# One layer's last two Strassen products, taken as a two-level unit

## The chip, the core and the metric

The kernel runs on one core of a Trainium2 chip. A core has a matmul engine (TensorE, `PE` in the profile, with its weight loads as `PEld`), a vector engine (VectorE, `DVE`), an activation engine (ScalarE, `ACT`), GpSimd (`POOL`) and a sync engine (`SP`), which in this kernel issues nearly all DMAs. Each engine runs its own instructions in order, and semaphores tie the engines together. The metric is the time of one launch in microseconds (us), as the median of several runs; a profiled execution gives the trace.

## The reference

Linear attention, then a block that mixes with Fourier transforms and a feed-forward layer, all in float32 (8 sequences of 576 tokens, 512 wide):

```python
def _attn_ref(q, k, v):                       # 8 heads of 64
    q_s = softmax(q, axis=-1); k_s = softmax(k, axis=2)
    kv = np.einsum('bhsd,bhse->bhde', k_s, v)
    return np.einsum('bhsd,bhde->bhse', q_s, kv)

def _moe_ref(x, w_ch1, w_ch2):                # w_ch1 512 x 2048, w_ch2 2048 x 512
    mixed = np.real(np.fft.fft(np.fft.fft(x, axis=1), axis=2))
    u = x + mixed
    un = (u - mean(u)) / np.sqrt(var(u) + 1e-06)
    return u + np.maximum(un @ w_ch1, 0.0) @ w_ch2
```

## The kernel before

The tokens are worked through in nine groups of 512, called orders. Order 0 multiplies plainly. From order 1 on the two layers of the feed-forward part are multiplied by Strassen's scheme in Winograd's form: seven products of half-size blocks take the place of eight, and sums of blocks are made before (the left and the right sides) and after. The products are numbered as in `A_AT` and `B_AT`, which say which of the seven left and right blocks each takes, and run in the order `ORDER = (1, 6, 5, 7, 2, 4, 3)`. While order 1 runs through its layers, TensorE also does the attention and the Fourier mixing of later sequences, and the other engines norm the tokens of the group that follows (`norm`: statistics L1335 and L1336, scales L1354 and L1357, normed tokens L1373, transposes on VectorE L1396, their pieces laid out by ScalarE and GpSimd L1404, and the right sides L1410, L1414, L1419).

Order 1's second layer is `down`. Its left side is the hidden layer: 512 tokens by 2048, seven blocks (slots) of 256 tokens by 1024 in the tile `big`. Each product is 16 matmuls of 128x128 by 128x256 (L2055; two records each in the trace), into one of three PSUM banks: 1 and 2 into `ba`, 6, 7 and 4 into `bb`, 5 and 3 into `bc`. `strassen` reads the banks: after product 1 ScalarE copies `ba` to `s1` (L1529); after 6 and 7 VectorE makes `u2` and `u3` from `bb` and `s1` (L1528); after 7, 2, 4 and 3 it adds a bank into a quarter of the tokens' tile x (L2070). GpSimd adds `s1`, `u2` and `u3` into x as well (L2065). So product 2 ends with the x add from `ba`, product 4 with that from `bb`, product 3 with that from `bc`.

The right side is seven combinations of the layer's weights, each a chunk of 1 MB loaded from DRAM (`w2s`) into a ring of four buffers in `big` (L490). `used(n)` frees chunk n and issues the load of chunk n + 4. Behind order 1's seven chunks in this ring come the first-layer chunks of order 2 (`w1s`, 896 KB each).

Orders 2 and later use a second level of Strassen in this layer (`deep_down`): products are taken in pairs, a unit, and each product is seven sub-products of 4 matmuls of 128x128 by 128x128 (L1938). The second combinations of the weights that this needs are made once, during order 1: for each product m but 1, `deepen` takes m's chunk, makes four sums (weights 4 and 1 on VectorE, 5 and 6 on GpSimd, L1818) into a spare place, and stores seven blocks to DRAM (`w2d`, 256 KB each, L1824): the three raw ones at once, the four sums six steps later. The spare place is in turn the gap behind the hidden layer (`gap`) and the slot of the product that has just been done.

The order of the work is a list. Every step is recorded with a time in a unit of its own (one product of this layer is 8 units), the list is sorted by these times, and each engine gets its instructions in that order; so a step written earlier comes earlier on its engine's queue, whatever it then waits for. In the layer, `deepen` starts at 8 for product 6, 12 for 5, 24 for 7, 28 for 2, 40 for 4 and 44 for 3. The products fill units 0 to 56, and order 2 starts at 56 (`UP`). The stores of x follow the x adds (`store`).

Of the kernel before, what the change touches and what calls it, by code (L numbers as in the profile page):

```python
# [52 lines left out]
HD = D // 2  # L53
# [26 lines left out]
ORDER = (1, 6, 5, 7, 2, 4, 3)  # L80
# [4 lines left out]
UP, TWICE = NP * len(ORDER), 8 + 6 * len(ORDER)  # L85
# [39 lines left out]
def at(t, script):  # L125
    return [(t + dt, step) for dt, step in script]
# [17 lines left out]
class _Block:  # L144
# [1365 lines left out]
            second.append(steps)  # L1510
        return first, second

    def strassen(self, product, step, out, early=lambda *a: []):

        nc, V = self.nc, self.nc.vector
        box = {}

        def bank(n):  # L1520
            box[n] = self.ps.tile([P, 2, HD], F32, tag=n, name=n)

        def temp(n):
# [4 lines left out]
        plus = lambda t: V.tensor_tensor(out=temp(t), in0=box["bb"][:], in1=box["s1"][:], op=ALU.add)  # L1528
# [508 lines left out]
    def down(self, g, order):  # L2037
        if order > 1:
            return self.deep_down(g, order)
        nc, V = self.nc, self.nc.vector  # L2040
        h = [self.hpairs(p) for p in range(NP)]
        steps, t = [], 4 * 2
        for k, m in enumerate(ORDER):
            if m != 1:
                spare = [self.hblock(A_AT[ORDER[k - 1]], a, b) for a in range(2) for b in range(2)]
                n = self.base[order] + NP + k
                steps += at(t * k - 4 * (k % 2 == 0), self.deepen(m, n, spare if k % 2 else [self.gap(i) for i in range(4)]))

        def product(m, bank, first):
            n = self.base[order] + NP + ORDER.index(m)  # L2050

            def run(i, q):
                w = self.stream[n]
                for p in range(4 * q, 4 * q + 4):
                    nc.tensor.matmul(bank()[:, i, :], lhsT=h[p][:, A_AT[m], i * P:(i + 1) * P], rhs=w[:, p, :],  # L2055
                                     start=first and i == 0 and p == 0, stop=p == NP - 1,
                                     skip_group_check=True)
                if (i, q) == (1, 1):
                    self.used(n)
            return [lambda i=i, q=q: run(i, q) for i in range(2) for q in range(2)]  # L2060

        def early(i, j, t):
            u, d = i - 1 if (i, j) != (1, 2) else 0, j - 1
            x = lambda: self.xs[g, u][:, :, d * HD:(d + 1) * HD]
            return [(0, lambda: nc.gpsimd.tensor_tensor(out=x(), in0=x(), in1=t()[:], op=ALU.add))]  # L2065

        def out(u, d, store):
            def run(bank, t):
                x = lambda: self.xs[g, u][:, :, d * HD:(d + 1) * HD]
                steps = [(0, lambda: V.tensor_tensor(out=x(), in0=bank()[:], in1=x(), op=ALU.add))]  # L2070
                for c in range(2 * store):
                    steps += at(15 + c, self.store(g, c, u, lambda c=c: self.xpart(g, c, u)))
                return steps
# [55 lines left out]
def kernel(ctx: ExitStack, tc: tile.TileContext, q, kT, v, w1, w2, ft,  # L2129
# [3 lines left out]
    ups = lambda order: 3 * UNIT + 2 * len(SHORT) * (NP // 2) if order in WIDE else UP  # L2133
# [61 lines left out]
    first, second, both = 46.9, 56, 77  # L2195
    steps = blk.opening(fetch, converted)
# [3 lines left out]
    t = first + second  # L2200
    for i, some in enumerate(down):
        steps += at(t + 1.2 * i, some)
# [93 lines left out]
```

## Time and profile before

| | before |
|---|---|
| median of 3 runs | 1002.66 us (1002.32 to 1003.45) |
| the profiled execution | 1004.02 us, its span 1002.1 us |
| TensorE busy | 990.0 us, 99% of the span |
| VectorE / ScalarE / GpSimd busy | 746.5 / 500.1 / 506.0 us |
| order 1's second layer on TensorE | from 229.75 us to 283.93 us |
| DMA | 240.32 MB, mean 240 GB/s |

A row of a timeline has the start in us from the start of the span, the length in us, the engine, the line, the operation, what is written from what, shapes, how many instructions of the same kind follow each other, and in brackets how long the engine stood idle before and what ended it. A row of several spans from the first's start to the last's end. Rows of windows give, for a stretch, the busy time and the number of instructions of PE, PEld, DVE, ACT and POOL, then the granted clock, the DMA share and GB/s. A row of waits has the total, how often, and the longest. `SPq` is the queue that issues DMAs.

### The profile page before, as it was taken

The numbers are of one execution on the slowest core, as the hardware profiler recorded it, in microseconds if no ns is written. First come the engines' busy times: TensorE is split into PE (matmuls) and PEld (weight loads), VectorE is DVE, ScalarE is ACT, GpSimd is POOL, SyncE is SP. The second block draws the span as 40 slices with busy tenths as digits, with TensorE's granted clock in tenths as the row PEclk, the third lists the DMA queues.
The fourth block names the chain that finished last, engine by engine and source line by source line (L and its number), as shares of the span: only waits on it lengthen the run. The fifth ranks groups of instructions, "written<-read, shape, count | busy, mean of one in ns | idle before, by whom it ended". The sixth has DMA issues, their size and how long they took to land.

```text
span 1002.1 us, 20374 instructions
## 1 busy us (share of the span) xinstructions
PE 990.0 (99%) x7754; PEld 856.9 (86%) x7754; DVE 746.5 (74%) x1402; ACT 500.1 (50%) x1290; POOL 506.0 (50%) x498
## 2 busy tenths in 40 slices
PE   8999999999999999999999999999999999999998
PEld 6845464888888899889988998899888999999997
DVE  6898899666765887678756886678657866895793
ACT  5585643872468228842775267724782243251310
POOL 4263420357535637664656556564647398352610
PEclk9999999999999999999999999999999999999999
DMA  9987499687989666975769577947656874677473
GB/s 301 261 282 245 161 253 339 199 245 224 332 295 270 225 233 224 253 256 202 265 196 241 210 263 246 260 175 260 231 174 230 311 251 153 251 268 246 151 268 140
DMA packets 128040, 240.32 MB, mean 240 GB/s; under 512 B 24312, under 2 KB 92152, under 8 KB 117448
## 3 DMA queue, kind: packets, MB, share of 16 engines
q1 hardware_dynamic: 127576, 238.51, 73.0%
q8 instruction: 61, 1.00, 0.4%
q14 instruction: 35, 0.29, 0.1%
q10 hardware_dynamic: 288, 0.26, 0.1%
q0 software_dynamic: 80, 0.26, 0.1%
HBM read 203.87 MB, written 39.06 MB: 242 GB/s over the span
## 4 chain that ended last, share of the span: by engine, by line
PE 87%; DVE 7%; DMA 2%; ACT 2%; issue 1%; SPq 0%; POOL 0%; DVEq 0%; POOLq 0%
PE bb L1560 12%; PE bb L1938 10%; PE ba L1560 8%; PE bc L1560 8%; PE ba L1938 7%; PE bc L1938 7%; PE bb L1888 4%; PE bc L1493 2%; PE bb L2055 2%; PE two L854 2%; PE one L769 2%; PE two L1221 1%; PE two L1278 1%; PE ba L1493 1%; PE ba L1716 1%; PE bc L2055 1%
## 5 line engine op out<-in xcount | busy, mean ns | idle before, releaser
L1560 PE MATMUL bb<-unT,big 128*128 128x256 f32 x576 | 137.8, 381 | 0.0
L1560 PEld LDWEIGHTS bb<-unT,big 128*128 128x128 f32 x576 | 108.4, 190 | 15.6 <-DVE u L1528 0.5
L831 ACT ACTIVATE qT<-q 32x128 f32<-32x128 f32 x384 | 117.9, 307 | 5.9 <-DVE q L821 0.7
L1938 PE MATMUL bb<-big 128*128 128x128 f32 x832 | 101.8, 276 | 0.2 <-DVE u L1945 0.2
L1938 PEld LDWEIGHTS bb<-big 128*128 128x128 f32 x832 | 97.1, 192 | 1.0 <-DVE u L1945 1.0
L1560 PE MATMUL ba<-unT,big 128*128 128x256 f32 x384 | 93.7, 383 | 0.7 <-DMA big<-w1s 0.7
L1560 PE MATMUL bc<-unT,big 128*128 128x256 f32 x384 | 91.2, 380 | 0.1
L1868 POOL TENSOR_TENSOR x<-x,big 128x512 f32<-128x512 f32 x45 | 60.7, 1362 | 45.9 <-DVE big L1945 19.7
L1572 ACT ACTIVATE big<-big 128x512 f32<-128x512 f32 x72 | 44.7, 628 | 78.2 <-DVE big L1571 71.6
L1560 PEld LDWEIGHTS bc<-unT,big 128*128 128x128 f32 x384 | 72.5, 190 | 10.4 <-DVE big L1571 0.5
L1528 DVE TENSOR_TENSOR u<-bb,s 128x512 f32<-128x512 f32 x50 | 34.2, 683 | 63.3 <-PE bb L1560 46.3
L1560 PEld LDWEIGHTS ba<-unT,big 128*128 128x128 f32 x384 | 71.3, 190 | 11.4 <-DMA big<-w1s 0.8
L1938 PE MATMUL ba<-big 128*128 128x128 f32 x648 | 80.1, 276 | 0.0
L1864 DVE TENSOR_TENSOR big<-big 128x512 f32<-128x512 f32 x95 | 78.1, 847 | 0.0
L1938 PEld LDWEIGHTS ba<-big 128*128 128x128 f32 x648 | 75.9, 192 | 0.8
L818 POOL TENSOR_TENSOR q<-q,qm 128x512 f32<-128x512 f32 x24 | 25.8, 1074 | 90.6 <-DVE qm L813 56.9
L1404 POOL COPY unT<-unT 32x256 f32<-32x256 f32 x98 | 43.5, 444 | 46.6 <-DVE unT L1396 42.3
L1404 ACT COPY unT<-unT 32x256 f32<-32x256 f32 x126 | 50.7, 402 | 29.8 <-DVE unT L1396 28.0
L415 POOL TENSOR_TENSOR big<-big 128x512 f32<-128x512 f32 x24 | 30.5, 1270 | 66.6 <-ACT big L1572 66.6
L1938 PE MATMUL bc<-big 128*128 128x128 f32 x400 | 48.9, 275 | 0.0
L1888 PE MATMUL bb<-big 128*128 128x256 f32 x208 | 47.7, 379 | 0.0
L1938 PEld LDWEIGHTS bc<-big 128*128 128x128 f32 x400 | 46.8, 192 | 0.0
(457 smaller groups left out, 2252.4 us busy)
## 6 DMA issues: line engine op xcount, KB each, us to landing
big<-w2d SPq DMA_DIRECT2D x68, 1024.0 KB
big<-w1s SPq DMA_DIRECT2D x64, 896.0 KB
big<-w2s SPq DMA_DIRECT2D x14, 1024.0 KB
big<-in_w_dram SPq DMA_DIRECT2D x21, 512.0 KB
w2d<-big SPq DMA_DIRECT2D x42, 256.0 KB
kb<-in_kT_dram SPq DMA_DIRECT2D x28, 320.0 KB
q<-in_q_dram SPq DMA_DIRECT2D x28, 256.0 KB
vt<-in_v_dram SPq DMA_DIRECT2D x84, 80.0 KB
```

Source lines behind the costliest of these rows:

```text
L415: e1.tensor_tensor(out=to(4), in0=at(2), in1=at(3), op=ALU.add)
L831: nc.scalar.activation(to[t, i * Q:i * Q + Q], one, ACT.Exp)
L1404: copy(to, of)
L1493: nc.tensor.matmul(po[:], lhsT=h[:, f, i * P:(i + 1) * P], rhs=self.w2sb[:, f, :], start=(f == 0), stop=(f == NF - 1))
L1528: plus = lambda t: V.tensor_tensor(out=temp(t), in0=box["bb"][:], in1=box["s1"][:], op=ALU.add)
L1560: nc.tensor.matmul(bank()[:, i, :], lhsT=w[:, WA_AT[m], k * P:(k + 1) * P], rhs=self.unT[g][:, B_AT[m], k, :], start=first and i == 0 and ...
L1572: (0.8, lambda: nc.scalar.activation(hp(i), hp(i), ACT.Relu))]
L1864: (engine or e).tensor_tensor(out=to(o), in0=to(x), in1=to(y), op=op)
L1868: E.tensor_tensor(out=x, in0=x, in1=tile(m), op=ALU.add)
L1888: nc.tensor.matmul(box[name][:, i, :], lhsT=h[p][:, A_AT[m], i * P:(i + 1) * P], rhs=self.stream[n][:, p, :], start=p == 0 and (m != 1 or ...
L1938: nc.tensor.matmul(box[place(unit, n)][:, i, :], lhsT=own(m)(A_AT[n])[:, f, :], rhs=w[:, r // 2, r % 2 * P:r % 2 * P + P], start=first and ...
L2055: nc.tensor.matmul(bank()[:, i, :], lhsT=h[p][:, A_AT[m], i * P:(i + 1) * P], rhs=w[:, p, :], start=first and i == 0 and p == 0, stop=p == ...
```

## The change

Products 4 and 3 of order 1's second layer are taken together as one two-level unit, `last_pair`, of the kind that later orders have: 7 sub-products by 2 by 4 matmuls of 128x128 by 128x128. Its right side is what `deepen` has made for products 4 and 3, still in its spare place, and the raw blocks of the chunks; its left side gets four sums for each of the two products, written into slots 0 and 5 (`dead`). Sub-products 1 and 2 go into `bb`, 6, 7 and 4 into `ba`, 5 and 3 into `bc`. The results are written over the hidden layer's slots 3 and 6, and GpSimd adds them into x (`into`).

The weights' sums of `deepen` start at 8 (product 6), 12 (5), 18 (7), 25 (4), 28 (2) and 33 (3), with other spare places. The x adds from `bb` and `bc` that ended products 4 and 3 come right after product 7, without those products. Chunks 4 and 3 are freed at the end of the unit. Order 2 starts two units earlier, and the stores of x have times of their own. On VectorE the sums 4, 4, 5, 5 of the left side stand before the x add from `ba`.

```diff
-    def strassen(self, product, step, out, early=lambda *a: []):
+    def strassen(self, product, step, out, early=lambda *a: [], order=ORDER):
...
-        for m in ORDER:
+        if 4 not in order:
+            ends[7] += at(0.1, out[2, 1](get("bb"), None) + out[1, 2](get("bc"), None))
+        for m in order:
...
-        steps, t = [], 4 * 2
+        steps, t, spare = [], 4 * 2, {}
         for k, m in enumerate(ORDER):
             if m != 1:
-                spare = [self.hblock(A_AT[ORDER[k - 1]], a, b) for a in range(2) for b in range(2)]
-                n = self.base[order] + NP + k
-                steps += at(t * k - 4 * (k % 2 == 0), self.deepen(m, n, spare if k % 2 else [self.gap(i) for i in range(4)]))
+                dead, start = {6: (1, 8), 5: (0, 12), 7: (6, 18), 4: (5, 25), 2: (0, 28), 3: (7, 33)}[m]
+                spare[m] = [self.hblock(A_AT[dead], a, b) if dead else self.gap(2 * a + b) for a in range(2) for b in range(2)]
+                steps += at(start, self.deepen(m, self.base[order] + NP + k, spare[m]))
...
-        return steps + self.strassen(product, 2, {(1, 1): out(0, 0, False), (2, 1): out(1, 0, True),
-                                                  (2, 2): out(1, 1, False), (1, 2): out(0, 1, True)}, early)
+        for c in range(4):
+            steps += at((62.5 if c < 2 else 70.5) + c % 2, self.store(g, c % 2, c < 2, lambda c=c: self.xpart(g, c % 2, c < 2)))
+        return steps + at(t * 5, self.last_pair(g, order, spare)) + self.strassen(
+            product, 2, {(1, 1): out(0, 0), (2, 1): out(1, 0), (2, 2): out(1, 1), (1, 2): out(0, 1)}, early, ORDER[:5])
+
+    def last_pair(self, g, order, spare):
+        nc, V, G = self.nc, self.nc.vector, self.nc.gpsimd
+        unit, steps, box = (4, 3), [], {}
+        base = self.base[order] + NP
+        dead = {4: A_AT[1], 3: A_AT[6]}
+        place = {1: "bb", 2: "bb", 6: "ba", 7: "ba", 4: "ba", 5: "bc", 3: "bc"}
+        chunk = {m: base + ORDER.index(m) for m in unit}
...
+        def product(n, i):
+            m, name = unit[i], place[n]
+            first = i == 0 and n in (1, 6, 5)
+            if first:
+                box[name] = self.ps.tile([P, 2, P], F32, tag=name, name=name)
+            for f in range(4):
+                nc.tensor.matmul(box[name][:, i, :], lhsT=a_at(m, A_AT[n])[:, f, :], rhs=b_at(m, B_AT[n])[:, f, :],
+                                 start=first and f == 0, stop=f == 3, skip_group_check=True)
...
+        def ends(n):
+            first, last = (A_AT[m] for m in unit)
+            out = lambda j: self.hpairs(j)[:, first:last + 1:last - first, 0:P]
+            of = place[n]
+            if n == 1:
+                nc.scalar.copy(temp("s1"), box[of][:])
+            if n == 6:
+                plus(temp("u2"), of, "s1")
+            if n == 7:
+                plus(temp("u3"), of, "s1")
+                plus(out(3), "bc", "u3")
+            if n == 2:
+                nc.scalar.copy(out(0), box[of][:])
+            if n == 4:
+                plus(out(2), of, "s1")
+            if n == 3:
+                plus(out(1), of, "u2")
...
+        for (o, x, y, e, op), times in zip(((4, 2, 3, V, ALU.add), (5, 4, 0, V, ALU.subtract), (2, 0, 2, V, ALU.subtract), (6, 1, 5, G, ALU.subtract)),
+                                           ((-4, -3), (-2, -1), (2, 3), (4, 5))):
+            steps += [(t, lambda m=m, a=(o, x, y, e, op): a_step(m, *a)) for m, t in zip(unit, times)]
+        for k, n in enumerate(ORDER):
+            steps += [(2 * k + j, lambda n=n, j=j: product(n, j)) for j in range(2)] + [(2 * k + 1.5, lambda n=n: ends(n))]
+        steps += [(13.6 + 0.1 * i, lambda m=m: self.used(chunk[m])) for i, m in enumerate(unit)]
+        return steps + [(14.6, lambda: into(1, 0, 4)), (16.2, lambda: into(0, 1, 3))]
...
-        t += ups(order) + (TWICE if order > 1 else UP)
+        t += ups(order) + (TWICE if order > 1 else UP - 2)
```

More of the change, by code (lines that the diff above doesn't have):

```diff
@@ L2065, in early, with out @@
             return [(0, lambda: nc.gpsimd.tensor_tensor(out=x(), in0=x(), in1=t()[:], op=ALU.add))]
-        def out(u, d, store):
+        def out(u, d):
             def run(bank, t):
                 x = lambda: self.xs[g, u][:, :, d * HD:(d + 1) * HD]
[L2070 to L2073, printed above, removed]
-            return run
@@ L2077, in down @@
-        return steps + self.strassen(product, 2, {(1, 1): out(0, 0, False), (2, 1): out(1, 0, True),
-                                                  (2, 2): out(1, 1, False), (1, 2): out(0, 1, True)}, early)
+                return [(0, lambda: V.tensor_tensor(out=x(), in0=bank()[:], in1=x(), op=ALU.add))]
+            return run
+        for c in range(4):
+            steps += at((62.5 if c < 2 else 70.5) + c % 2, self.store(g, c % 2, c < 2, lambda c=c: self.xpart(g, c % 2, c < 2)))
+        return steps + at(t * 5, self.last_pair(g, order, spare)) + self.strassen(
+            product, 2, {(1, 1): out(0, 0), (2, 1): out(1, 0), (2, 2): out(1, 1), (1, 2): out(0, 1)}, early, ORDER[:5])
@@ new lines, in last_pair, with a_at, b_at, a_step @@
+    def last_pair(self, g, order, spare):
[5 more added lines that the diff above has]
+        chunk = {m: base + ORDER.index(m) for m in unit}
+        def a_at(m, i):
+            return self.hblock(dead[m], *((0, 1), (1, 0), (1, 1))[i - 4]) if i > 3 else self.hblock(A_AT[m], i // 2, i % 2)
+        def b_at(m, i):
+            return spare[m][(1, 4, 5, 6).index(i)] if i in (1, 4, 5, 6) else \
+                self.stream[chunk[m]][:, i // 2 * 4:i // 2 * 4 + 4, i % 2 * P:i % 2 * P + P]
+        def a_step(m, o, x, y, e, op):
+            e.tensor_tensor(out=a_at(m, o), in0=a_at(m, x), in1=a_at(m, y), op=op)
+        def product(n, i):
[6 more added lines that the diff above has]
+                                 start=first and f == 0, stop=f == 3, skip_group_check=True)
+        def temp(n):
+            box[n] = self.work.tile([P, 2, P], F32, tag=n, name=n, bufs=1)
+            return box[n][:]
+        def plus(out, name, t):
+            V.tensor_tensor(out=out, in0=box[name][:], in1=box[t][:], op=ALU.add)
+        def ends(n):
[15 more added lines that the diff above has]
+                plus(out(1), of, "u2")
+        def into(u, d, m):
+            x = self.xs[g, u][:, :, d * HD:(d + 1) * HD].rearrange("p c (e n) -> p c e n", n=P)
+            G.tensor_tensor(out=x, in0=x, in1=self.hblock(A_AT[m], 0, 0).rearrange("p (c e) n -> p c e n", c=2), op=ALU.add)
+        for (o, x, y, e, op), times in zip(((4, 2, 3, V, ALU.add), (5, 4, 0, V, ALU.subtract), (2, 0, 2, V, ALU.subtract), (6, 1, 5, G, ALU.subtract)),
[5 more added lines that the diff above has]
+        return steps + [(14.6, lambda: into(1, 0, 4)), (16.2, lambda: into(0, 1, 3))]
```

## The prediction

> **What bounds the kernel now.** I read the page first (busy shares, slices, the chain that ended last), then the waits of TensorE, then the timelines of TensorE, VectorE, GpSimd and the DMA queue round order 1's second layer.
>
> ```profile
> PE 990.0 (99%) x7754; PEld 856.9 (86%) x7754; DVE 746.5 (74%) x1402; ACT 500.1 (50%) x1290; POOL 506.0 (50%) x498
> PE   8999999999999999999999999999999999999998
> PE 87%; DVE 7%; DMA 2%; ACT 2%; issue 1%; SPq 0%; POOL 0%; DVEq 0%; POOLq 0%
> ```
>
> TensorE is busy 990.0 of 1002.1 us and carries 87% of the chain. So a microsecond of matmul time saved is a microsecond gained, and one of TensorE waiting is one lost, unless something after it gives way. The changed stage in TensorE's timeline (start, length; 32 records are one product, since each matmul of the code leaves two):
>
> ```profile
> 263.20 7.07 PE L2055 MATMUL ba<-big 128*128 128x256 f32 x32
> 270.11 7.07 PE L2055 MATMUL bb<-big 128*128 128x256 f32 x32
> 277.02 7.07 PE L2055 MATMUL bc<-big 128*128 128x256 f32 x32
> 283.93 1.89 PE L1560 MATMUL ba<-unT,big 128*128 128x256 f32 x8
> ...
> 365.15 1.95 PE L1938 MATMUL ba<-big 128*128 128x128 f32 x16
> 366.94 1.95 PE L1938 MATMUL bb<-big 128*128 128x128 f32 x16
> ```
>
> Product 2 (into `ba`) ends at 270.11, products 4 and 3 follow without a gap, and order 2 begins at 283.93. The last two rows are two-level work in order 2: 16 records in 1.79 us.
>
> **The change, part by part.** *TensorE.* Out go products 4 and 3, 283.93 - 270.11 = 13.82 us. In come 7 sub-products of 16 records at 1.79 us, 12.53 us. That is -1.3 us, with little doubt.
>
> *VectorE before the unit.* The first sub-product uses bank `bb`, the second (6) bank `ba`. Bank `ba` holds products 1 and 2 until VectorE has added them to x (`out(0, 0)`, the row at 270.31 below). In the changed order this add stands behind the hidden layer's first four sums (4 and 5 for each of products 4 and 3), behind the weights' two sums for product 3, and behind the x adds that now come early. TensorE reaches sub-product 6 at 270.11 + 1.79 = 271.90. So the question is when VectorE gets through. Its timeline before:
>
> ```profile
> 253.99 1.29 DVE L1818 TENSOR_TENSOR big<-big 128x512 f32<-128x512 f32 x2
> ...
> 263.40 0.69 DVE L1528 TENSOR_TENSOR u<-bb,s 128x512 f32<-128x512 f32 x1 [2.19 <-PE bb L2055]
> 265.48 0.69 DVE L2070 TENSOR_TENSOR x<-bc,x 128x512 f32<-128x512 f32 x1 [1.38 <-POOL x L2065]
> 266.09 1.29 DVE L1396 STREAM_TRANSPOSE unT<-eo 128x512 f32<-128x512 f32 x2
> 267.30 0.65 DVE L1335 BATCH_NORM_STATS2 st<-x 128x6 f32<-128x512 f32 x1
> ...
> 268.78 0.18 DVE L1336 BATCH_NORM_AGGREGATE mv<-st 128x2 f32<-128x6 f32 x1
> 269.33 0.17 DVE L1354 RECIPROCAL std<-std 128x2 f32<-128x2 f32 x1 [0.36 <-ACT std L1351]
> 269.53 0.16 DVE L1357 SCALAR_TENSOR_TENSOR mv<-mv,std 128x2 f32<-128x2 f32 x1
> 270.31 0.69 DVE L2070 TENSOR_TENSOR x<-ba,x 128x512 f32<-128x512 f32 x1 [0.62 <-PE ba L2055]
> ```
>
> The row at 265.48 waits for GpSimd's add of `u3`; two further x adds fit into that wait (263.40 to 265.48), so they cost nothing. Without any conflict a sum takes 0.60 to 0.65 (1.29 for two at 253.99). Then from 265.48: x add 0.61, two transposes 1.21, two weight sums 1.2, the statistics 1.66 (267.30 to 268.96), three hidden sums 1.9, the two small rows 0.36, one more sum 0.6, the x add of `ba` 0.69: it ends at 273.7. That is the floor: TensorE waits 1.8 us.
>
> GpSimd works beside it all that while, and rows show what that does:
>
> ```profile
> 249.32 1.27 POOL L2065 TENSOR_TENSOR x<-x,u 128x512 f32<-128x512 f32 x1 [3.53 <-DVE u L1528]
> 254.82 1.58 POOL L1818 TENSOR_TENSOR big<-big 128x512 f32<-128x512 f32 x1 [4.23 <-PE bc L2055]
> 256.61 4.59 POOL L1818 TENSOR_TENSOR big<-big 128x512 f32<-128x512 f32 x3 [0.21 <-PE bc L2055]
> 264.18 1.27 POOL L2065 TENSOR_TENSOR x<-x,u 128x512 f32<-128x512 f32 x1 [2.98 <-DVE u L1528]
> 267.51 3.03 POOL L1404 COPY unT<-unT 32x256 f32<-32x256 f32 x7 [2.07 <-DVE unT L1396]
> 274.47 1.76 POOL L1818 TENSOR_TENSOR big<-big 128x512 f32<-128x512 f32 x1
> 891.72 4.86 POOL L1404 COPY unT<-unT 32x256 f32<-32x256 f32 x7 [3.81 <-DVE unT L1396]
> ```
> ```profile
> 250.00 0.87 DVE L1308 TENSOR_TENSOR x<-x,eo 128x257 f32<-128x257 f32 x1
> 274.42 2.37 DVE L1818 TENSOR_TENSOR big<-big 128x512 f32<-128x512 f32 x2 [1.00 <-DMA w2d<-big]
> 892.96 1.68 DVE L1864 TENSOR_TENSOR big<-big 128x512 f32<-128x512 f32 x2
> ```
>
> A VectorE sum of two SBUF tensors that meets a GpSimd sum waits for its end: the one at 250.00 ended at 250.87, just after GpSimd's at 250.59, and the second of the pair at 274.42 ended at 276.79, 0.56 after GpSimd's (276.23). Beside GpSimd's short copies (891.72) the two sums at 892.96 took 1.68, where two alone took 1.29: 0.2 more each, so about 0.8.
>
> Now GpSimd after the change. The weights' sums for products 7 and 4 are made earlier, so six of its sums, not four (254.82, 256.61), stand between its add of `u2` (ends 250.59) and its add of `u3`. The first can start at about 251.2. Six at 1.27, each letting one or two VectorE sums through at about 0.55, and a wait near 258 for product 4's weights, end at about 264.4; the add of `u3` then ends near 265.7, 0.25 later than now. From there, with the conflicts: x add and first transpose to 266.9; product 3's first weight sum to 267.6; transpose; its second weight sum meets GpSimd's sum (267.7 to 269.0) and ends at 269.5; statistics to 271.1; the first hidden sum meets GpSimd's second (269.8 to 271.1), ends at 271.65; two hidden sums beside copies, 0.8 each, to 273.2; the small rows to 273.5; the last to 274.2; the x add to 274.9. TensorE waits 274.9 - 271.9 = 3.0 us. I take that, between the floor of 1.8 and a ceiling of 4.1 (each of GpSimd's six sums lets two VectorE sums through, 0.5 more; and every copy, 0.43 by the row at 267.51, holds one of three sums up for its whole length, 0.2 more for each).
>
> [...]
>
> *The unit itself.* Two stretches of the kernel before (length; busy time of PE, PEld, DVE, ACT, POOL; clock, DMA share, GB/s):
>
> ```profile
> 260.00:270.00 10.00, 10.00 (x48) 8.81 (x47) 5.62 (x13) 3.69 (x8) 4.73 (x8) 1.00 1.10 324
> 270.00:284.00 14.00, 14.00 (x67) 12.32 (x66) 8.17 (x11) 8.47 (x18) 10.95 (x14) 1.00 1.08 364
> ```
>
> The waits after that are covered by the shifted TensorE: `u2` is read from `ba` while sub-product 5 runs in `bc` (1.79 us for one add of half a tile), `u3` while 2 runs. The sums 2 on VectorE and 6 on GpSimd are needed only in sub-products 7 and 3, 3.6 and 9 us after the restart; the first two of them are the closest, some 0.6 us ahead, because the second pair of transposes with its two activations stands before them. ScalarE gets two short copies more and has room (8.47 busy of 14.00). GpSimd loses four weight sums among its copies of the normed tokens and gets two hidden sums, so order 2's right-hand side is not later. The two new adds of results into x (1.27 each, as at 264.18) and the stores come once order 2 has begun, and nothing on the path waits for them. Without that cover each would cost its own length.
>
> *The DMA queue.* All 42 stores of second combinations stay, but more of them are issued ahead of order 2's second weight chunk. The sizes by the page, and the queue's issues:
>
> ```profile
> big<-w1s SPq DMA_DIRECT2D x64, 896.0 KB
> big<-w2s SPq DMA_DIRECT2D x14, 1024.0 KB
> w2d<-big SPq DMA_DIRECT2D x42, 256.0 KB
> ```
> ```profile
> 256.49 0.32 SPq L490 DMA_DIRECT2D big<-w2s  x1
> 256.86 9.93 SPq L1824 DMA_DIRECT2D w2d<-big  x10
> 266.88 0.64 SPq L490 DMA_DIRECT2D big<-w1s  x1
> 267.62 1.83 SPq L1824 DMA_DIRECT2D w2d<-big  x4
> 269.87 0.32 SPq L490 DMA_DIRECT2D big<-w1s  x1
> ```
>
> By the stretches above the queue is full (DMA shares over 1, 324 to 364 GB/s). After the change 3 stores precede the load of 256.49, and 21 instead of 14 stand between it and the second chunk. Bytes from 256.49 on: 24 stores of 0.262 MB, 1.05 MB, two chunks of 0.918 MB, 9.2 MB; at those rates 25 to 28 us, so it lands at 282 to 285. Order 2 needs it 0.86 us after its start (half of 8 records). With a start at 285.6 that is 286.4, hidden. Without VectorE's wait the start would be 282.6, the need 283.5, and up to 1.5 us would show. Chunks 3 and 4 are freed only at the unit's end, but are wanted 12 us later.
>
> **The sum.** -1.3 + 3.0 = +1.7 us. The profiled execution took 1004.02 (span 1002.1), so against it that is 1005.7; it stood 1.4 above the median of 1002.66, so I forecast 1002.66 + 1.7 = 1004.4. The bounds: -1.3 + 1.8 = +0.5 and -1.3 + 4.1 = +2.8.
>
> **Rivals.** *Slower by over 0.2%* (2.0 us; about what a measurement here can tell from no change): VectorE's queue loses more to GpSimd. Place: the ten entries before the x add of `ba`. It decides from a wait of 3.3 us; at the ceiling it gives 1005.5. For it: both engines' rows above are slowed wherever they meet. Against: a copy costs only 0.2. 24%.
>
> *TensorE's clock falls during the wait.* Its longest wait once it runs, from the view of waits:
>
> ```profile
> PE ba L1481 <- ACT eo L1340: 0.9, 1, 0.9
> ```
>
> No row shows a wait of 3 us, so the rows neither bear this out nor exclude it. If TensorE came back at half its pace for as long as it had stood, 3.0 us, 1.5 us would be added: 1005.9. 6%. [...]
>
> *The weight chunk decides.* From a landing at 286.8 on (0.86 after a start that is 2.0 later than now) it makes the kernel over 0.2% slower, and each further us costs one; at 288, 1005.9. The rows say 282 to 285. 4%.
>
> *VectorE is in time after all*, as its busy share suggests (5.62 of 10.00 us): TensorE's -1.3 stands, cut by the chunk (282 to 285 against a need at 283.5) to about -0.5 and 1002.2. Against: the floor counts only measured lengths in an order that the engine must keep. 5%.
>
> The change does what it says: 112 records for 64, and 1.79 per 16 is measured in the same kind of unit.
>
> **How the numbers follow.** The forecast holds 57%; its own range is 1003.1 to 1004.6. Slower by over 0.2%: 24 + 6 + 4 = 34%. Within 0.2%: 57 + 5 = 62%. Faster by over 0.2%: nothing here saves 2 us, and 4% are left for a gain that no row shows. The range reaches from the in-time case to just above the clock case, 1002.2 to 1006.1.
>
> **What would show it.** In the changed kernel TensorE idles 2 to 4 us before the second group of 16 records (bank `ba`), ended by VectorE's x add; the seven groups otherwise follow at 1.79; order 2 begins near 285.6 and has no wait for `w1s`. Wrong if that idle time is under 1.5 us, if matmuls after it are slower than 1.79 per 16, or if a DMA ends a wait of TensorE.

## The result and the profile after

The changed kernel takes 1007.25 us (median of 6 runs, 1005.42 to 1007.79), the kernel before 1002.91 in the runs beside it (6 runs, 1002.32 to 1003.51): a ratio of 1.0041, 95% interval 1.0028 to 1.0054, or 4.1 us more (2.8 to 5.4). The forecast was 1.7 us more, and 1007.25 lies above its range. Of the six runs the four with a mean granted clock of TensorE of 0.998 or less took 1006.65 to 1007.79, the two at 1.00 took 1005.42 and 1007.00.

From the page of the changed kernel (busy times, and the chain that ended last); its profiled execution took 1007.72, span 1005.8:

```profile
PE 991.3 (99%) x7802; PEld 859.5 (85%) x7802; DVE 754.6 (75%) x1413; ACT 500.6 (50%) x1292; POOL 513.4 (51%) x502
PE 82%; DVE 9%; ACT 4%; DMA 2%; SPq 1%; issue 1%; POOL 1%; POOLq 0%; DVEq 0%
```

TensorE is as busy as before (991.3 against 990.0), but 3.7 us of span were added, and VectorE now has 9% of the chain (7% before). TensorE's timeline in the changed stage:

```profile
263.92 7.07 PE L2057 MATMUL ba<-big 128*128 128x256 f32 x32
270.83 1.95 PE L2105 MATMUL bb<-big 128*128 128x128 f32 x16
275.70 3.03 PE L2105 MATMUL ba<-big 128*128 128x128 f32 x16 [2.92 <-DVE x L2072]
278.52 2.61 PE L2105 MATMUL bc<-big 128*128 128x128 f32 x16
280.97 1.95 PE L2105 MATMUL ba<-big 128*128 128x128 f32 x16
282.76 1.95 PE L2105 MATMUL bb<-big 128*128 128x128 f32 x16
...
288.12 1.89 PE L1562 MATMUL ba<-unT,big 128*128 128x256 f32 x8
```

Two things went wrong, one behind the other. TensorE waited for VectorE's x add from `ba`, as forecast. Then the next two groups, the same 16 records that take 1.79 us elsewhere, took 2.82 and 2.45 us from start to start. The stretches (length; busy time of PE, PEld, DVE, ACT, POOL; granted clock, DMA share, GB/s) say why:

```profile
262.00:276.00 14.00, 11.08 (x61) 9.86 (x60) 13.15 (x23) 5.99 (x13) 11.44 (x13) 1.00 1.10 332
275.50:276.50 1.00, 0.80 (x7) 0.83 (x8) 0.69 (x3) 0.96 (x3) 0.55 (x2) 1.00 1.15 344
276.50:278.00 1.50, 1.50 (x9) 1.50 (x9) 1.50 (x3) 1.44 (x4) 0.74 (x1) 0.50 1.16 347
278.00:279.50 1.50, 1.50 (x9) 1.50 (x9) 1.00 (x2) 1.45 (x5) 1.38 (x3) 0.50 1.11 400
279.50:281.00 1.50, 1.50 (x14) 1.50 (x13) 0.00 (x0) 1.47 (x4) 1.40 (x3) 0.86 1.10 427
```

TensorE's granted clock is 0.50 from 276.5 on. In the last row a mean of 0.86 over 1.5 us means 0.42 us at half clock, so it lasted until 279.92: 3.4 us. The first row shows the other half of the story: VectorE is busy 13.15 of 14.00 us up to the point at which TensorE may go on.

The account, by starts: from the end of product 2 (270.83) to order 2 (288.12) it takes 17.29 us, where before it took 13.82: +3.47. Of that the unit's records give 12.53 - 13.82 = -1.29, the wait 275.70 - 270.83 - 1.79 = +3.08, and half clock 2.82 + 2.45 - 2 x 1.79 = +1.69. The sum is +3.48. Of the 4.1 us of the runs the rest, 0.6, lies within their interval and is not located. It is not behind the unit: from order 2's start to the end the kernel before takes 718.2 us, 717.4 in a second profile, and the changed kernel 717.7. Ahead of it the profiled executions of all kernels here scatter by more: product 2 starts between 261.3 and 263.9 us.

### The profile page after: what moved, and what is told of

Same layout as the page of the kernel before. It is cut to its first block, busy times and chain, and to the rows that moved or that the text cites. A ratio compares the mean times of both kernels' runs of the same rounds, so it can differ in the third digit from the quotient of the medians.

```text
span 1005.8 us, 20491 instructions
## 1 busy us (share of the span) xinstructions
PE 991.3 (99%) x7802; PEld 859.5 (85%) x7802; DVE 754.6 (75%) x1413; ACT 500.6 (50%) x1292; POOL 513.4 (51%) x502
## 4 chain that ended last, share of the span: by engine, by line
PE 82%; DVE 9%; ACT 4%; DMA 2%; SPq 1%; issue 1%; POOL 1%; POOLq 0%; DVEq 0%
PE bb L1562 11%; PE bb L1940 10%; PE ba L1562 8%; PE bc L1562 7%; PE ba L1940 7%; PE bc L1940 7%; PE bb L1890 4%; PE bc L1493 2%; ACT qT L831 2%; PE two L854 2%; PE one L769 1%; PE ba L1493 1%; PE ba L1718 1%; PE one L1718 1%; PE bb L1718 1%; PE bc L1718 1%
## 5 line engine op out<-in xcount | busy, mean ns | idle before, releaser
L1404 POOL COPY unT<-unT 32x256 f32<-32x256 f32 x98 | 46.4, 474 | 45.1 <-DVE unT L1396 40.8
```

The lines of the kernel that those rows point to most:

```text
L1404: copy(to, of)
```

## The experiments

The theory after this: the loss is the wait for VectorE's queue, plus TensorE's clock, which falls because of the wait. Rivals: the slow records come from traffic and not from having waited; the moved sums and stores cost time by themselves; VectorE and GpSimd have no room in this stretch, so that a wait removed comes back elsewhere. Each experiment is compared with the kernel before as it ran beside it (medians of 1002.6 to 1003.2).

### The sums' new times alone

The kernel before, with the new times and places of `deepen` and without the unit:

```diff
-                spare = [self.hblock(A_AT[ORDER[k - 1]], a, b) for a in range(2) for b in range(2)]
...
+                dead, start = {6: (1, 8), 5: (0, 12), 7: (6, 18), 4: (5, 25), 2: (0, 28), 3: (7, 33)}[m]
+                spare = [self.hblock(A_AT[dead], a, b) if dead else self.gap(2 * a + b) for a in range(2) for b in range(2)]
+                steps += at(start, self.deepen(m, self.base[order] + NP + k, spare))
```

> The kernel before with the new places and times of the weights' second combinations alone: no two-level unit, products 4 and 3 as they were, the stores in their old positions for x. Wait-and-clock theory: nothing here makes TensorE wait, 1002.9 within 0.5. Rival 2 (moved sums and stores cost by themselves): 1003.8, with a wait of TensorE somewhere that the kernel before doesn't have.

Measured: ratio 1.0003 (0.9994 to 1.0012), no change. Its waits of TensorE have one, ended at 286.83 us, that the kernel before lacks at this place (a wait of 0.7 us for `w1s` in its first profile stands at 539 us):

```profile
PE ba L1560 <- DMA big<-w1s: 1.4, 1, 1.4
```

The moved sums are not the loss. (This kernel leaves the stores and the adds into x where they were; for those the 717.7 us behind the unit, given above, speak.) The row is the weight chunk that the prediction said would show "up to 1.5 us" if VectorE made nobody wait: it does, with 1.4. In the runs it is not to be told from nothing.

### TensorE busy through its wait

The changed kernel, the first sub-product issued twice:

```diff
-        def product(n, i):
+        def product(n, i, again=False):
...
-            if first:
+            if first and not again:
...
+        steps += [(t, lambda j=j: product(1, j, True)) for t, j in ((1.1, 0), (1.2, 1))]
```

> The changed kernel, with the first sub-product (16 records, 1.79 us) issued twice, so that TensorE works through most of its wait; VectorE's work is untouched, TensorE's only grows. Wait-and-clock theory: the idle time falls from 2.9 to 1.1 us, sub-product 6 starts when it did, the clock stays at 1.00, and the unit's other groups take 1.79 us: 1.8 us under the changed kernel, 1005.4, with more work. Rival 1 (slow by traffic, not by having waited): the two groups after the wait stay slow, and the time is the changed kernel's, 1007.2.

Measured: 1005.68, ratio 1.0029 (1.0020 to 1.0038); the changed kernel stood at 1.0041. TensorE's timeline, and a stretch of the same execution:

```profile
269.88 3.73 PE L2105 MATMUL bb<-big 128*128 128x128 f32 x32
274.74 2.02 PE L2105 MATMUL ba<-big 128*128 128x128 f32 x16 [1.13 <-DVE x L2072]
276.60 1.95 PE L2105 MATMUL bc<-big 128*128 128x128 f32 x16
```
```profile
274.50:276.50 2.00, 1.76 (x16) 1.79 (x17) 1.68 (x4) 1.92 (x5) 0.78 (x3) 1.00 1.15 345
276.50:278.50 2.00, 2.00 (x20) 2.00 (x19) 1.46 (x3) 1.93 (x6) 1.88 (x3) 1.00 1.18 356
```

The kernel does 1.79 us more work, and from product 2's end to order 2 it takes 15.71 us (269.88 to 285.59) against 17.29. The medians of the runs differ by 1.6 us the same way, the ratios by 0.0012, and the intervals of these overlap; the granted clock is 0.999 or 1.00 in all 11 runs, where four of six had a lower one. Sub-product 6 starts as late after product 2 as in the changed kernel (274.74 - 269.88 = 4.86; 275.70 - 270.83 = 4.87), so the gain is not in the wait; the clock stays at 1.00 at the same DMA load (345 and 356 GB/s), and the groups take 1.86 and 1.79. Slowness by traffic falls with this.

### Half of that, and where the clock begins to fall

```diff
+        steps += [(t, lambda j=j: product(1, j, True)) for t, j in ((1.1, 0),)]
```

> The changed kernel with only the first half of the first sub-product issued twice (8 records, 0.9 us): TensorE's idle time is about 2.0 us, between the 1.1 that left the clock at 1.00 and the 2.9 that halved it; sub-product 6 starts when it did, so all that differs is the clock. Without a fall of the clock it takes what the run with the whole sub-product took, 1005.6; with it, the changed kernel's 1007.2. If the fall depends on where the wait lies against windows of a fixed length (half clock lasted 3.4 us in the changed kernel, twice that in the two kernels with waits of 4.0 and 5.9), single runs fall on either side: some with a granted clock of 0.998 or less and 1.5 us longer.

Measured: 1.0034 (1.0021 to 1.0047), wait 2.03 us. Two of its five runs have a mean granted clock of 0.998 or less and take 1007.6 and 1007.9; the other three take 1005.4 to 1006.4. A wait of 2 us halves the clock in some executions and not in others. All runs of kernels with the unit, sorted by TensorE's longest wait in the unit and just behind it (from the profiled execution of each; runs at a mean clock of 0.998 or less, out of all):

| longest wait | 0.6 | 1.1 | 1.1 | 2.0 | 2.0 | 2.1 | 2.5 | 2.6 | 2.9 (the change) | 3.0 | 3.3 | 4.0 | 5.9 |
|---|---|---|---|---|---|---|---|---|---|---|---|---|---|
| runs | 0 of 7 | 0 of 5 | 0 of 11 | 2 of 5 | 2 of 5 | 2 of 5 | 5 of 7 | 5 of 5 | 4 of 6 | 4 of 5 | 5 of 6 | 5 of 5 | 5 of 5 |

One of the 63 runs of the kernel before that stand beside the experiments has such a mean too.

The traces also show what decides at 2 us. In the changed kernel's trace the mean clock is 0.50 from 276.497 to 279.910 us and 1.00 just before and just behind: half clock lasts 3.413 us. In each of the nine profiled executions in which the clock fell here, it fell once more at the end of the work, and the two moments are a whole number of 3.413 us apart: in the changed kernel 1003.54 - 276.50 = 727.04 us, 213 times (both read from the mean clock of stretches of 0.5 us). So in these traces the clock goes by stretches of 3.41 us that run on through the whole execution; in the other profiles the end of the work gives their place. Cut along them, each of the ten stretches at full clock in which TensorE stood for 2.03 us or more was followed by half clock, and none (the end of the work apart) in which it stood for 1.84 or less (2.03 in this kernel, 1.84 ahead of the fall in the faulty version below). First two such stretches of this kernel, then two of the last version below, whose wait of 1.99 us is divided between them:

```profile
272.57:275.98 3.41, 1.38 (x12) 1.22 (x12) 3.11 (x7) 2.46 (x5) 2.88 (x5) 1.00 1.00 293
275.98:279.39 3.41, 3.41 (x18) 3.41 (x17) 2.51 (x4) 3.27 (x10) 2.46 (x3) 0.50 1.15 346
```
```profile
275.99:279.40 3.41, 1.96 (x18) 1.77 (x16) 3.41 (x3) 0.00 (x0) 2.42 (x2) 1.00 1.10 365
279.40:282.82 3.42, 2.88 (x25) 2.88 (x26) 2.19 (x6) 1.91 (x5) 1.69 (x5) 1.00 1.03 379
```

The stretches begin at other moments in each execution (276.50 is a boundary in the changed kernel, 275.98 here), so it is chance how a wait falls on them. An estimate from the bound between 1.84 and 2.03: a wait of 2.0 us halves the clock in 45% of the executions, one of 2.9 in 70%, one of 3.9 or more always; the table has 6 of 15, 4 of 6 and 10 of 10.

### Two hidden sums earlier

```diff
-                                           ((-4, -3), (-2, -1), (2, 3), (4, 5))):
+                                           ((-14, -3), (-13, -1), (2, 3), (4, 5))):
```

> The changed kernel with two of the four hidden sums some 10 us earlier and nothing else moved: the x add comes about 1.3 us sooner, and TensorE's wait falls from 2.9 to about 1.6 us. This asks from which wait on the clock falls. If it does not at 1.6 us: 1007.25 - 1.3 - 1.8 = 1004.1. If any wait of that order is followed by half the clock: 1005.9. Rival 1 (traffic): 1005.9 too, but with slow matmuls also in the run that fills the wait.

Measured: 1008.90, 1.0057 (1.0043 to 1.0071): worse. VectorE's timeline, GpSimd's, and TensorE's:

```profile
258.82 3.44 DVE L2097 TENSOR_TENSOR big<-big 128x512 f32<-128x512 f32 x2
...
266.63 0.68 DVE L1528 TENSOR_TENSOR u<-bb,s 128x512 f32<-128x512 f32 x1
```
```profile
258.43 3.27 POOL L1820 TENSOR_TENSOR big<-big 128x512 f32<-128x512 f32 x2 [4.16 <-DVE big L1820]
```
```profile
276.34 3.76 PE L2105 MATMUL ba<-big 128*128 128x128 f32 x16 [4.01 <-POOL unT L1404]
279.89 2.98 PE L2105 MATMUL bc<-big 128*128 128x128 f32 x16
```

The two sums, 0.65 each when alone, took 3.44 beside two sums of GpSimd, and everything behind them moved: `u3` is made at 266.63 without any idle time before it, and the x add ends at 276.2, just before sub-product 6 starts (the bracket puts the wait down to GpSimd's copies, but it is the x add that frees the bank). There was no room at 259 either. TensorE's wait grew to 4.0 us, and here half clock lasted twice as long:

```profile
274.90:276.40 1.50, 0.06 (x1) 0.09 (x1) 1.29 (x3) 1.45 (x4) 1.36 (x4) 0.60 1.15 348
...
280.40:281.90 1.50, 1.50 (x9) 1.50 (x9) 0.23 (x1) 1.47 (x4) 1.44 (x2) 0.50 1.09 427
281.90:283.40 1.50, 1.50 (x15) 1.50 (x15) 0.00 (x0) 1.46 (x4) 1.38 (x3) 0.96 1.05 444
```

By the same arithmetic as above it runs from 275.2 to 282.0, 6.8 us: two of the stretches of 3.41 us. TensorE stood for 1.13 us of the first.

A second version of this moved the x add of `ba` ahead as well. Its edit was faulty: the x add (`-1.7`) stands ahead of the last quarter of product 2, so x lacks that quarter, and the quarter waits for the add.

> The cause of TensorE's wait is taken away: two of the four hidden sums move some 10 us ahead, the x add of bank ba stands ahead of the other two. Wait-and-clock theory (the changed kernel lost 2.9 us in the wait for VectorE's x add and, right after it, about 1.8 us at half the granted clock): a wait of at most 0.6 us is left, no matmul of the unit runs slow, and of the 1.3 us that the unit saves at least 0.7 arrive: 1002.2 (1001.6 to 1002.6), 5 us under the changed kernel. Rival 1 (the slow matmuls after the wait come from traffic in SBUF, not from having waited): they stay, 1.8 us more, 1004.0. Rival 2 (the moved sums and stores cost some 0.9 us by themselves, outside this stage): 1003.1.

Measured: 1010.56, a wait of 5.9 us inside product 2, and 6.8 us of half clock again. It tells nothing of the cure that it was meant for; it adds the last column of the table.

### One weight sum later

Product 3's second weight sum (1.41 us at 268.87 in the changed kernel, beside a sum of GpSimd) goes behind the x add:

```diff
-        return [(0, lambda: minus(V, 4, 1, 0)), (1, lambda: minus(V, 1, 3, 1)), (1, lambda: minus(G, 5, 3, 4)),
+        return [(0, lambda: minus(V, 4, 1, 0)), (6.6 if m == 3 else 1, lambda: minus(V, 1, 3, 1)), (1, lambda: minus(G, 5, 3, 4)),
```

> The changed kernel with one instruction moved on VectorE: product 3's second weight sum (1.41 us at 268.9, stretched by GpSimd's sum) goes behind the x add of ba; sub-product 7 needs it only at 277. If the wait is the length of VectorE's queue, the x add comes 1.4 us sooner, the wait is 1.5 us and the clock stays at 1.00: 1007.25 - 1.4 - 1.8 = 1004.0. If a wait of 1.5 us halves the clock now and then, single runs lie 1.7 above that. If GpSimd's sums take the room (the queue is held up by the next meeting instead), 0.7 us come back and the wait is 2.2.

Measured: 1005.58, 1.0028 (1.0017 to 1.0040), wait 2.5 us. The third of the expected outcomes, with a wait somewhat longer than its 2.2: the hidden sums now come earlier, meet GpSimd's second sum, and lose 1.0 of the 1.4 us again (VectorE, then GpSimd):

```profile
269.13 3.23 DVE L2097 TENSOR_TENSOR big<-big 128x512 f32<-128x512 f32 x3
```
```profile
268.94 1.27 POOL L1820 TENSOR_TENSOR big<-big 128x512 f32<-128x512 f32 x1
```

In the changed kernel the same three took 2.26.

### Another order of the sub-products

Sub-product 2 needs neither `ba` nor a new sum; in a bank of its own it can run second. The x add of `ba` also moves ahead of two hidden sums (not shown):

```diff
-        place = {1: "bb", 2: "bb", 6: "ba", 7: "ba", 4: "ba", 5: "bc", 3: "bc"}
+        place = {1: "bb", 2: "bc", 6: "ba", 7: "ba", 4: "ba", 5: "bb", 3: "bb"}
...
-        for k, n in enumerate(ORDER):
+        for k, n in enumerate((1, 2, 6, 5, 7, 4, 3)):
```

> The unit's sub-products in the order 1, 2, 6, 5, 7, 4, 3: sub-product 2, which needs none of the new sums and not bank ba, runs second (in bc), the one that needs ba third, and the x add of ba stands ahead of two of the hidden sums. VectorE's work before that point stays as it was. Wait-and-clock theory: TensorE reaches bank ba at 274.4 in the changed kernel's time and waits 0.6 us at most, the clock stays at 1.00, the unit's saving of 1.3 us arrives nearly whole: 1002.75 - 1.3 + 0.3 = 1001.8 (1001.3 to 1002.4). Chunk theory (the kernel with the times alone waited 1.4 us for order 2's second weight chunk): the saving goes into that wait instead, which ends near 284, 1.1 us or more: 1002.8 to 1003.3. If the moved sums and stores cost 0.9 by themselves: 1002.7 without any such wait.

Measured: 1009.63, 1.0060 (1.0047 to 1.0073). The wait at `ba` is down to 0.55 us, and a hidden sum on VectorE ends it; but another wait took its place (TensorE, then VectorE):

```profile
283.99 3.79 PE L2105 MATMUL ba<-big 128*128 128x128 f32 x16 [3.28 <-DVE u L2113]
```
```profile
282.91 0.69 DVE L1410 TENSOR_TENSOR unT<-unT 128x512 f32<-128x512 f32 x1 [4.31 <-POOL unT L1404]
283.52 0.42 DVE L2113 TENSOR_TENSOR u<-ba,s 128x256 f32<-128x256 f32 x1
```

The later end of sub-product 7 had fallen behind a sum of the normed tokens in VectorE's in-order queue, which waits 4.3 us for GpSimd's copies.

The same kernel with three more sums ahead of the x add ran beside it:

```diff
+        steps += [(-1.95, lambda: a_step(4, 4, 2, 3, V, ALU.add))] * 3
```

> The reordered kernel with one of the hidden sums made three times more (with the same result) ahead of the x add of ba: VectorE's queue is longer by some 2.2 us and nothing else changes. If VectorE's queue is what TensorE waits for, the wait is 2.5 us (2.0 to 3.0): 1001.8 + 2.2 = 1004.0 without a fall of the clock, 1005.7 with one. If the wait were set by something else (a DMA, GpSimd), the time stays at the reordered kernel's.

Measured: 1010.96, 1.0080 (1.0067 to 1.0093). The wait at `ba` is 2.57 us instead of 0.55, 2.0 more for three sums of VectorE: its queue does set that wait. The other wait shrank to 2.3, and the clock fell in all five runs; in the profiled one it fell at 274.94 and again at 285.18, three stretches of 3.41 us later.

With sub-product 7 written ahead of that sum (`zip((0, 2, 4, 5, 6, 10, 12), (1, 2, 6, 5, 7, 4, 3))` as starts):

> The reordered kernel, with sub-product 7 and its end written ahead of the normed tokens' sum of 128x512 in VectorE's queue, as in the changed kernel (in the reordered one that sum, which waits until 282.91 for GpSimd's copies, stood ahead of u3, and TensorE waited 3.3 us for u3). Wait-and-clock theory: that wait goes, waits of 0.55 and 0.3 us are left, the clock stays at 1.00: -1.3 + 0.9 = -0.4 against the kernel before, 1002.8 (1002.0 to 1003.5). Chunk theory: up to 1 us more, with a wait for w1s at order 2's start.

Measured: 1005.85, 1.0030 (1.0019 to 1.0042); no clock below 0.999. The 3.3 us are gone, but four waits of VectorE stay, 0.55, 0.32, 0.52 and 0.60 us. From product 2's end to order 2 it takes 15.48 us, 1.66 more than before. That is 2.95 above the 12.53 of the records, where the brackets of the four waits add up to 1.99: by starts each wait costs 0.2 us more than its bracket shows, and the group after it up to 0.1.

Both edits together:

> The untangled kernel with the late sum: nothing of VectorE's queue that sub-product 6 needs is late. Wait-and-clock theory: waits of 0.3 us or less in the unit, clock 1.00, order 2 starts 1.0 to 1.3 us sooner than in the kernel before: 1003.0 - 1.2 = 1001.8 (1001.2 to 1002.4), the first version that beats it. Chunk theory: order 2 starts at 282.7 and needs its second weight chunk at 283.6; it lands near 284 to 285, and 0.4 to 1.4 us of the gain are lost there: 1002.2 to 1003.2.

Measured: 1006.29, 1.0035 (1.0022 to 1.0049), clock 1.00 in all runs; waits of 0.15, 1.11, 0.52 and 0.58 us. (Its profiled execution is the shortest of the five, 1003.75; the stage takes 15.88 us in it.) What the late sum gave at `ba` it took at `u2`. Neither the expected gain nor the chunk: VectorE is late four times.

### Every known wait taken out

Sub-product 4 in a bank of its own, `u2` and two sums ahead of the second transposes; the late sum and the x add's earlier place stay (only the banks and the starts are shown, against the changed kernel):

```diff
-        place = {1: "bb", 2: "bb", 6: "ba", 7: "ba", 4: "ba", 5: "bc", 3: "bc"}
+        place = {1: "bb", 2: "bc", 6: "ba", 7: "ba", 4: "bc", 5: "bb", 3: "bb"}
...
+        for n, start, end in ((1, 0, 0.1), (2, 0.15, 0.6), (6, 0.3, 0.5), (5, 0.7, 0.9), (7, 2, 3), (4, 6, 8), (3, 9, 13.5)):
```

> The late sum and the order 1, 2, 6, 5, 7, 4, 3, with sub-product 4 in a bank of its own (bc, added to u3 afterwards, so that it doesn't wait until VectorE has read ba) and two more sums and u2 ahead of the second transposes. Wait-and-clock theory: each of the four waits of the run before last (0.15, 1.1, 0.5 and 0.6 us) loses its cause; the unit's records come within 12.5 to 13.0 us, clock 1.00, order 2 starts 0.8 to 1.3 us sooner than in the kernel before, and the time is 1003.0 - 1.0 = 1002.0 (1001.3 to 1002.8). Saturation theory (VectorE and GpSimd have no room in this stretch, so each wait removed brings out the next): the transposes that were put off hold up GpSimd's copies and its sum of the normed tokens, order 2's first or second product waits for that 1 us or more, and the time is 1003 to 1004.

Measured: 1007.15, 1.0046 (1.0032 to 1.0060). Now six of the seven sub-products run almost without a wait, and what they saved is lost right behind them (TensorE, then VectorE):

```profile
269.07 1.95 PE L2105 MATMUL bb<-big 128*128 128x128 f32 x16
...
280.28 1.06 PE L2105 MATMUL bb<-big 128*128 128x128 f32 x8
282.01 1.16 PE L2105 MATMUL bb<-big 128*128 128x128 f32 x8 [0.68 <-POOL big L2097]
283.34 1.99 PE L1562 MATMUL ba<-unT,big 128*128 128x256 f32 x8 [0.17 <-POOL unT L1404]
287.40 2.82 PE L1562 MATMUL bb<-unT,big 128*128 128x256 f32 x8 [2.06 <-DVE big L2113]
```
```profile
274.34 1.28 DVE L2097 TENSOR_TENSOR big<-big 128x512 f32<-128x512 f32 x2
...
283.93 2.99 DVE L747 TENSOR_REDUCE km<-kb 128x4 f32<-128x640 f32 x4
286.84 0.41 DVE L2113 TENSOR_TENSOR big<-bb,u 128x256 f32<-128x256 f32 x1
```

Six groups in 280.28 - 269.07 = 11.21 us is 1.87 each. Then a sum of GpSimd is late, and the unit's last result stands behind four reductions of VectorE; the clock falls as well, in order 2 (a mean of 0.70 from 287.3 to 290.0 us and of 0.66 from there to 292.6). The unit's stretch is down to 14.27 us, 0.45 more than before, but what follows takes 722.0 us instead of 717.4 to 718.2: a wait removed in the unit came back behind it, and the time lies above both expected ranges.

The last version puts GpSimd's two sums ahead of its copies, that result ahead of the reductions, and seven stores behind the weight chunk (only the sums' starts are shown, against the changed kernel):

```diff
-                                           ((-4, -3), (-2, -1), (2, 3), (4, 5))):
+                                           ((-4, -3), (-1.8, -1), (-0.2, -0.1), (-0.05, -0.04))):
```

> The last kernel with its two remaining causes of waits taken out: the sums 6 on GpSimd come before its copies of the normed tokens (it idled 3.7 us there), the end of sub-product 3 stands ahead of four reductions in VectorE's queue, and seven stores of second combinations are issued after order 2's second weight chunk instead of before it. If the changed kernel lost its time to waits and to the clock after them and to nothing else, the unit's saving shows at last: records within 12.5 to 12.9 us, no wait over 0.3 in the unit or at order 2's start, clock 1.00, 1002.8 - 1.1 = 1001.7 (1001.0 to 1002.4). If the stretch is saturated, another wait of 1 us or more takes their place: 1003 to 1004.5.

Measured: 1007.14, 1.0047 (1.0033 to 1.0060), above the range for a saturated stretch as well. Again another wait (TensorE, VectorE, GpSimd), and in order 2 two more, of 1.33 and 0.34 us, for VectorE:

```profile
279.94 2.05 PE L2105 MATMUL ba<-big 128*128 128x128 f32 x16 [1.99 <-DVE u L2113]
```
```profile
275.52 3.43 DVE L2097 TENSOR_TENSOR big<-big 128x512 f32<-128x512 f32 x2
```
```profile
275.14 3.27 POOL L2097 TENSOR_TENSOR big<-big 128x512 f32<-128x512 f32 x2
```

The two VectorE sums that took 1.28 in the run before took 3.43, because GpSimd's sums were moved to where they are. The saturation theory holds for every order tried here. That no order could do it is not shown.

Beside it ran the same kernel with four more sums ahead of the x add (`* 4` in the line shown above):

> The kernel beside it with one hidden sum made four times more (with the same result) in VectorE's queue ahead of the x add of ba: about 2.8 us (2.4 to 3.4) of VectorE work and nothing else, which TensorE can only wait for. Wait alone: 2.5 us more than the kernel beside it. Wait and clock: half clock for 3.4 us or a multiple of that after the wait, 1.7 us more or twice that, 4.2 to 5.5 us in all, in most of its runs.

Measured: 1009.26, 1.0061, so 2.1 us more than its neighbour. The wait at `ba` is 2.95 us, followed by a group of 3.44 us instead of 1.79 (clock 0.998 or less in four of five runs), and the wait of 1.99 is down to 0.2. With wait and clock 4.2 to 5.5 was expected, with the wait alone 2.5, which is nearer. By the traces the stage is 2.43 us longer: 2.8 for the wait at `ba`, 1.6 for half clock, and -2.0 for the neighbour's own wait, which this one covers. So the price of wait and clock is there, but the sum of the runs does not show it by itself.

### The kernel before once more

> The kernel before once more, for a second profile: whether the waits of its first profiled execution (0.67 us for w1s at 539, 0.7 before L854, 0.18 near 890) are there each time. The first execution took 1004.02, 1.3 above its median; if these waits come and go, this one takes 1002.7 within 0.7 and lacks some of them.

Measured: 1002.91. The wait for `w1s` at 539 is not among its waits, and from product 2's end to order 2 it takes 13.82 us again. So the stage is steady, and the rest moves by a microsecond from one execution to the next; the first profiled execution of the kernel before was one of its longer ones.

## Why the prediction was wrong

**The step that failed** is the rival "TensorE's clock falls during the wait". The prediction named it, worked out 1.5 us for it, and wrote that the rows "neither bear this out nor exclude it". It then gave it 6%, without a reason for so little, and left it out of the sum. It happened in four of the six runs, the profiled one among them, and cost 1.69 us there. The prediction's own sign of being wrong came with it: two groups of 16 records took 2.82 and 2.45 us instead of 1.79. With the measured 1.7 us for it the prediction's own sum is -1.3 + 3.0 + 1.7 = +3.4, against the +3.47 of the trace. The range reached just past the clock case with the forecast wait (1005.9), not past longer waits with it. A cost that no row excludes has two ends, and the range has to reach to the upper one. With the ceiling of the wait and the half clock as measured here (2.8 + 1.7 = 4.5 on 1002.7) it would have ended at 1007.2, still just short of 1007.25; the last part of the miss is in the base and in the 0.6 us that are not located.

The 1.5 us took half pace to last as long as TensorE had stood, 3.0 us; the traces do not show that. They show half clock for 3.4 us after a wait of 2.9 in the changed kernel, and for 6.8 after some longer waits in others. In the changed kernel the 3.4 us before the fall, 273.1 to 276.5, hold 0.8 us of matmuls by the row of 275.50; 2.03 us of standing within a stretch were enough in another kernel. No run here shows why the clock goes by such stretches.

**The wait of VectorE** was right, in kind and in size: 3.0 us forecast, 3.08 by starts, and the run with three more sums shows that VectorE's queue makes such a wait. Step by step: the x add was put 4.8 us behind product 2's end (274.9 - 270.11); its row

```profile
274.87 0.68 DVE L2072 TENSOR_TENSOR x<-ba,x 128x512 f32<-128x512 f32 x1
```

ends 4.72 behind it (275.55 - 270.83). The weight sum that meets GpSimd's was forecast at 1.3 (a transpose after 267.6 and the sum, to 269.5), it took 1.41; the three hidden sums, mostly beside copies, at 2.1 in all (271.1 to 273.2), they took 2.26. In the changed kernel that is 0.75 a sum, mostly beside GpSimd's copies, against 1.7 beside its sums in the last version (3.43 for two): here copies cost VectorE little. That each holds a sum up for its whole length, as the ceiling of 4.1 us took it, no row shows.

**TensorE's 12.53 us** were right where the clock was whole: groups 1.79 apart.

**What lies behind the unit** was right: no further wait in the changed kernel. It was right because TensorE was late, so this was in part luck: with TensorE nearer to its time, in the other orders, `u2`, `u3`, GpSimd's sums and the last result are each late in one or another. The prediction's "some 0.6 us ahead" for the closest of them was the sign of it.

**The weight chunk** was priced right for TensorE on time (up to 1.5 us forecast, 1.4 seen with the times alone) and hidden in the changed kernel, as forecast.

**The base.** 1002.66, the median of three runs, has become 1002.6 to 1003.2 in the runs since, and 1002.91 beside the changed kernel. That is 0.25 us of the 1.15 by which the time lies above the range.

## What to carry to other kernels

Where TensorE is the bound, a stage with less matmul time but more sums must be counted on the engines that make the sums as well: here the unit saves 1.3 us of TensorE and fills VectorE to 13.15 of 14.00 us (9.13 in the same stretch before), and each of the orders tried gave the saving back. Price a wait of TensorE of 2 us or more with the half clock that may follow (here in 39 of 54 runs with such a wait, by a mean clock of 0.998 or less), 1.7 us or up to 3.1 where it lasted twice as long, and not with its own length alone; in the traces 1.8 us of useless matmuls in the wait cost 1.6 us less than standing still. And sums placed side by side on VectorE and GpSimd take VectorE nearly as long as both together (3.43 us for two and two, where two alone take 1.28 on VectorE and one 1.27 on GpSimd), so that in this stretch moving one earlier or later was free only where the other engine had a gap too.

## What was not expected of the hardware

- By a mean granted clock of 0.998 or less, the clock fell after waits of 2.0 to 2.1 us in 6 of 15 runs, after 2.5 to 3.3 us in 23 of 29, and never in 23 runs with waits of up to 1.1 us.
- In the profiled executions in which it fell it stayed at half for 3.4 us after waits of 2.0 to 3.0 us, and for 6.8 us after those of 3.3, 4.0 and 5.9.
- In the traces the clock goes by stretches of 3.413 us that run on through an execution (213 of them lie between the two falls in the changed kernel): 2.03 us of standing within one were followed by half clock each time, 1.84 us were not. Half clock went on for a second stretch where TensorE stood for 0.68 us or more of the first (three executions), and ended after one where it stood for 0.37 or less (seven falls).
- Two VectorE sums that take 1.28 us alone took 3.43 beside two GpSimd sums of 3.27.
